# A linear-attention and mixer kernel: the order of the first batch, the pace of weight conversion, two clears and a small copy

## The chip, the cores and the metric

The kernel runs on one core of one Trainium2 chip. Its time is the device time of one execution in microseconds (us). The time before is the median of three executions; one further execution was taken by the profiler.

The engines go by their short names in the profile: PE is TensorE, PEld its weight loads, DVE VectorE, ACT ScalarE, POOL GpSimd, SP SyncE (here it only issues DMAs).

## The reference

Sizes: 4 batches, 8 heads, 768 steps, head dimension 48; model width 384, hidden width 1536, rank 32.

```python
f = 1.0 / (1.0 + np.exp(-f_logit))
for t in range(S):
    state = f[:, :, t, :, None] * state + np.einsum('bhd,bhe->bhde', k[:, :, t], v[:, :, t])
    y[:, :, t] = np.einsum('bhd,bhde->bhe', q[:, :, t], state)
# heads side by side: x has shape (batch, seq, 384)
h = x.transpose(0, 2, 1) @ U @ V
u = x + h.transpose(0, 2, 1)
out = u + np.maximum(u @ w_ch1, 0.0) @ w_ch2
```

The inputs q, k, v and f_logit are float32. The weights U, V, w_ch1 and w_ch2 are float64 and are turned into float32 on the chip.

## The kernel before

**Units.** The attention works in units of two heads; a batch has HP = 4 units, so units 0 to 3 are the first batch and there are NU = 16. A unit's 768 steps are 12 chunks of C = 64. Its front (`prepare`) makes decayed keys and queries; its rear (`attend`) has the pieces `kept` (transposes of the keys, L899, copied by ScalarE, L903), `spread` (the chunks' decays repeated, L909), `states` (sums of keys and values by chunk, L920, copied by ScalarE, L927), `scan` (the states one after the other, a VectorE scan, L942), `scores` (L872) and `mask` (VectorE, L885), `read` (queries by states into y, L959), and `inner` (masked scores by values into the same y, L977; then ScalarE copies y into x, L983).

**The two kinds of front.** In the first batch the five pieces of the front are: `gates` = logarithms (VectorE floor L730, ScalarE exp and ln L732 and L733), `read_back` = sums of them on TensorE (`log_sums`, L739), `keep` = three exponentials and a copy on ScalarE (L752 to L757), then `keys` and `queries` (transposes on TensorE, L709, and a VectorE product, L721). From unit 4 on, `gates` is a sigmoid (L763 or L771), `keep` a backward VectorE scan (L776) with a few 12-column operations behind it (L781 to L786), `read_back` a forward scan (L794). These scans read `fz`, in which the first column of each chunk and one more column at the end must be zero, and `starts`, which holds one value at the first column of each chunk and zeros elsewhere. In the first batch `fz` serves as scratch (its exponentials are kept there).

**Order.** TensorE, VectorE and ScalarE run the pieces in the order in which the code calls them, each engine in its own queue; up to `written.close()` SP's loads are in written order too. In the loop over n in the first batch a list of pieces is put together for each unit and called through. One call of a piece queues its instructions on every engine it uses. Two PSUM pools limit how far TensorE runs ahead: `ps_big` (3 buffers of two banks: transposes, scores, states, y, and the mixing products) and `ps_mm` (2 buffers of one bank: the mixer's products `pz` and `po`, and the low-rank products `ph`).

**Weights.** `weight_loader` gives four functions for each tile of float64 weights: the first issues its DMA; `halves` makes two ScalarE operations (L91, L92); `join` three VectorE operations (L98, L99, L100) and one GpSimd addition that writes the float32 tile (L101). `weights` holds U, two pieces of V (early = 3), 12 tiles of w_ch1 (called tiles 0 to 11 here) and 12 of w_ch2. `ahead_by` couples them: converting weight number i first issues the DMA of number i + 10.

**The mixer of the first batch.** After unit 3 come the low-rank products in two parts (`done`: the columns of units 0 to 2; `rest`: those of unit 3), the additions to x (`mix_of`, VectorE L197), transposes of x (`turn_of`, L279, L255), and 18 pieces `ch1` of 12 recorded matmuls each (L293, L267) that end in a ScalarE relu (L310). Piece (j, a) needs the w_ch1 tiles 2j and 2j + 1. The loop below runs the later pieces, converts weight tiles after each, and from i = 3 on adds one attention piece of the second batch:

```python
        for t in [starts] + fz:
            nc.vector.memset(t, 0.0)
        ...
        for i, (_, piece) in enumerate(start + m.firsts[1:]):
            piece()
            for f in loads[: (2, 1, 2, 1, 1, 0)[i] if i < 6 else 1]:
                loads.remove(f)
                f()
            if i >= EARLY:
                next(second)()
```

`busy` issues matmuls on a zero tile into a bank that nothing reads (L1068).

Of the kernel before, what the change touches and what calls it, by code (L numbers as in the profile page):

```python
# [111 lines left out]
def ahead_by(n, loads):  # L112


    def call(i):
        if i + n < len(loads):
            loads[i + n][0]()
        loads[i][1]()

    return [lambda i=i: call(i) for i in range(len(loads))]  # L120
# [396 lines left out]
def factored_path(ctx, tc, q, k, v, f_logit, moe_U, moe_V, moe_w_ch1, moe_w_ch2, out, ok):  # L517
# [4 lines left out]
    nc = tc.nc  # L522
    B, H, S, D = q.shape
    P = nc.NUM_PARTITIONS
    C = P // 2
# [111 lines left out]
    nc.vector.memset(ends, 0.0)  # L637
    nc.vector.memset(ends.rearrange("p (c t) -> p c t", t=C)[:, :, C - 1], 1.0)
    starts = other[:, 3, :]
    fz = [const.tile([P, S + 1], F32, name=f"fz{i}") for i in range(2)]  # L640

    kz = [const.tile([P, C + S], F32, name=f"kz{i}") for i in range(2)]
# [2 lines left out]
    least = const.tile([P, NU, NCH], F32, name="least")  # L645
# [14 lines left out]
    early = len(weights)  # L660
# [18 lines left out]
    def backwards(t, first, n):  # L679

        a = t[:, first : first + 1]
        return bass.AP(a.tensor, a.offset, [list(a.ap[0]), [-1, n]])
# [9 lines left out]
    def prepare(n):  # L692
# [4 lines left out]
        r, f = raw[n % 2], fz[n % 2]  # L697
# [76 lines left out]
        def keep():  # L774
            X = T["X"] = late[:, 4, :]
            nc.vector.tensor_tensor_scan(  # L776
                backwards(X, S - 1, S), backwards(f, S, S), backwards(ends, S - 1, S), 0.0,
                ALU.mult, ALU.add,
            )
            X0 = X.rearrange("p (c t) -> p c t", t=C)[:, :, 0]  # L780
            nc.scalar.copy(least[:, n, :], X0)  # L781
            X1 = two.tile([P, NCH], F32, name="X1")
            nc.vector.tensor_single_scalar(X1, X0, LEAST, ALU.max)
            nc.vector.reciprocal(starts.rearrange("p (c t) -> p c t", t=C)[:, :, 0], X1)
            whole = wholes[n % 2]
            nc.vector.tensor_tensor(whole[:, 1:NCH], T["f0"][:, 1:NCH], X0[:, 1:NCH], ALU.mult)  # L786
# [19 lines left out]
    def mixer(b):  # L806
        return Mixer(tc, b, x_tiles[b], U, V, w1, w2, sums if b else None, ident, blocks, out, two, three, zp, ps_big, ps_mm,
                     b == 0, z_all, room if b >= B - 2 else None, FEWER - (b - B + 2) * NCH // 4)
# [184 lines left out]
    def front(n, *names):  # L993

        if n >= NU:
            return []
        if n not in ahead:
            ahead[n] = dict(zip(("gates", "keep", "keys", "read_back", "queries"), prepare(n)))
        return [ahead[n].pop(nm) for nm in names]

    def rear(n, *names):

        if not 0 <= n < NU:
            return []
        if n not in here:
            here[n] = dict(zip(("kept", "states", "scan", "scores", "read", "inner", "mask", "spread"), attend(n)))
        return [here[n].pop(nm) for nm in names if nm in here[n]]
# [23 lines left out]
    def attention(pieces, portions, todo):  # L1031

        fill = Fill(todo, portions)
        for piece in pieces:
            fill()
            piece()
        fill.rest()

    def beside(pieces, n, calls):

        for i, piece in enumerate(pieces):
            yield piece
            for f in calls[:2] if i >= n else []:
                calls.remove(f)
                f()
        assert not calls
# [14 lines left out]
    with tc.manual_schedule(engines={nc.vector.engine, nc.scalar.engine}):  # L1061


        idle = ps_mm.tile([P, 512], F32, name="idle", tag="mm")

        def busy(n, cols=DM):
            for _ in range(n):
                nc.tensor.matmul(idle[:, 0:cols], lhsT=blank[:, 0:P], rhs=blank[:, 0:cols], start=True, stop=True)  # L1068

        written = ExitStack()  # L1070
        written.enter_context(tc.manual_schedule(engines={nc.sync.engine}))
        busy(3)
        for piece in front(0, "gates", "read_back", "keep"):
            piece()
        load(1, "k", "q")
        load(2, "f")
        load(1, "v")
        loads = ahead_by(early + FIRST + 1, weights)
        halves, join = [[w[i] for w in weights[:early]] for i in (2, 3)]
        done, rest = slice(0, 2 * (HP - 1) * D), slice(2 * (HP - 1) * D, DM)  # L1080

        def held():
            for i in range(2, FIRST, 2):
                t = zp.tile([P, NFC // 2, 2 * P], F32, name="zw").rearrange("p i t -> p (i t)")
                nc.scalar.copy(t[:, 0:1], x_tiles[0][:, 0, 0:1])
                spare.extend([t.bitcast(U64)[:, 0:WP], t.bitcast(U64)[:, WP : 2 * WP]])
            for load_w in weights[early + 2 : early + FIRST]:
                load_w[0]()
            load(HP, "f", "k", "q", "v")

        for n in range(HP):
            last = n + 1 == HP
            pieces = rear(n - 1, "scan") + (join[:1] if last else []) + front(n, "keys") + rear(n, "spread")
            pieces += rear(n - 1, "read") + front(n, "queries") + rear(n, "kept")
            if n == 0:
                pieces += [lambda: busy(1, 2 * P)] + front(1, "gates") + rear(0, "scores", "mask", "states")
            elif last:
                pieces += halves[1:2] + join[1:2] + rear(n - 1, "inner") + [held] + rear(n, "scores", "mask")
                pieces += halves[2:] + rear(n, "states", "scan") + join[2:]
            else:  # L1100
                pieces += rear(n - 1, "inner") + front(n + 1, "gates") + rear(n, "scores", "mask", "states")
            if n + 2 == HP:
                pieces += halves[:1]
            if not last:
                pieces += front(n + 1, "read_back", "keep")
            for piece in pieces:
                piece()
            if n == 0:
                load(2, "k", "q")
                load(3, "f")  # L1110
                load(2, "v")
            elif n == 1:
                weights[0][0]()
                load(3, "k", "q")
                for load_w in weights[1:early]:
                    load_w[0]()
                load(3, "v")
                for load_w in weights[early : early + 2]:
                    load_w[0]()
        m = mixer(0)  # L1120
        low_rank_of, added_up_of, mix_of, turn_of, ch1_of = m.some
        for load_w in weights[early + FIRST : early + FIRST + 4]:
            load_w[0]()
        load(HP + 1, "f", "k", "q", "v")
        written.close()
        low_rank_of(done)
        busy(2, 2 * P)
        loads[early]()
        for piece in rear(n, "read"):
            piece()  # L1130
        loads[early + 1]()
        added_up_of(done)
        for piece in rear(n, "inner"):
            piece()
        mix_of(done, range(0, NBL - 2, 2))
        low_rank_of(rest)
        mix_of(done, range(NBL - 2, NBL, 2))
        added_up_of(rest)
        turn_of(0, range(2))
        mix_of(rest)  # L1140
        ch1_of(0, 0, (0, 0), (0, 1))
        turn_of(0, range(2, NDC))
        ch1_of(0, 0, (1, 0), (1, 1))
        m.before[4][1]()
        ch1_of(0, 0, (0, 2), (1, 2))
        loads = loads[early + 2 :]
        loads.pop(0)()
        for t in [starts] + fz:
            nc.vector.memset(t, 0.0)

        start = m.before[5:]

        EARLY = 3
        second = chain(front(HP, "gates", "keep", "keys", "read_back", "queries"), steps(HP, 2 * HP + 1))
        for i, (_, piece) in enumerate(start + m.firsts[1:]):
            piece()
            for f in loads[: (2, 1, 2, 1, 1, 0)[i] if i < 6 else 1]:
                loads.remove(f)
                f()
            if i >= EARLY:  # L1160
                next(second)()
        for f in loads:
            f()
        n = len(m.seconds) // (NBL // 2)
        todo, after = m.seconds[:-n], m.seconds[-n:]

        attention(second, 12 + 10 * HP - (len(start) + len(m.firsts) - 1 - EARLY), todo)
        m = start_mixer(1, after)
        for f in to_sum:
            f()  # L1170
# [5 lines left out]
    pieces = beside(steps((B - 1) * HP + 1, NU + 1), 10 * (HP - 2), [lambda i=i: sum_of_w(i) for i in range(len(W_SUMS))])  # L1176
# [374 lines left out]
```

## Time and profile before

| | us |
|---|---|
| median of 3 executions (lowest, highest) | 484.69 (483.83, 487.08) |
| the profiled execution | 483.4 |
| its span, first to last instruction | 481.7 |
| PE busy | 462.5 (96%) |
| PEld busy | 399.2 (83%) |
| DVE busy | 345.8 (72%) |
| ACT busy | 180.7 (38%) |
| POOL busy | 36.1 (7%) |

A busy row counts an engine's instructions, not its waits. In a timeline line the two numbers in front are start and duration in us; what stands in square brackets is how long the engine sat idle before, and what released it. A line of the waits is: engine and operation that waited, what it waited for, total us, times, longest. A line of the stretches is: from and to, length, busy us of PE, PEld, DVE, ACT and POOL with instruction counts, the granted TensorE clock (1.00 is full), the DMA share and GB/s. A line of the DMA issues ends with the KB of each and the median us from issue to landing.

### The profile page before, as it was taken

Reading aid. Unit: us, or ns where it says so; the run is one execution under the profiler, and the core shown is the slowest. Engines: PE = TensorE matmul, PEld = TensorE weight load, DVE = VectorE, ACT = ScalarE, POOL = GpSimd, SP = SyncE. Lnnn points to the kernel's source line nnn. Section 1 sums busy time; section 2 is a strip of 40 time slices with the busy share of each in tenths; the row PEclk is TensorE's granted clock in tenths of the full one; section 3 lists DMA queues with packets and bytes.
Section 4 is the critical chain, followed back from the end, with each engine's and each line's share of the span. In section 5 each row is a group of like instructions: output and inputs, shape, how many; then the busy total and the mean of one; then the engine's idle time right before and its main releaser. Section 6 shows DMA issues by size and latency. Waiting matters only on the chain.

```text
span 481.7 us, 12787 instructions
## 1 busy us (share of the span) xinstructions
PE 462.5 (96%) x5551; PEld 399.2 (83%) x5551; DVE 345.8 (72%) x557; ACT 180.7 (38%) x339; POOL 36.1 (7%) x48
## 2 busy tenths in 40 slices
PE   7899979998999899999999999999999999999995
PEld 5786868885666468799899888899979999999995
DVE  4567686798999755757766646997896886858642
ACT  5675665663444313424342414542321311212200
POOL 2002254443000000000000000000000000000000
PEclk9999999998999999999999999999999999999999
DMA  9979996657787521253426200100000000000001
GB/s 145 153 134 252 217 207 130 157 134 108 109 125 113 95 42 26 26 75 72 64 28 114 43 30 4 29 3 20 17 1 1 33 2 18 18 0 34 1 33 39
DMA packets 158679, 34.34 MB, mean 71 GB/s; under 512 B 149206, under 2 KB 157078, under 8 KB 158614
## 3 DMA queue, kind: packets, MB, share of 16 engines
q1 hardware_dynamic: 158614, 33.44, 37.6%
q8 instruction: 45, 0.74, 0.7%
q14 instruction: 20, 0.16, 0.1%
HBM read 28.70 MB, written 4.72 MB: 69 GB/s over the span
## 4 chain that ended last, share of the span: by engine, by line
PE 77%; DVE 11%; ACT 3%; issue 3%; SPq 2%; DMA 2%; POOL 1%; DVEq 0%; POOLq 0%; ACTq 0%
PE pw L356 26%; PE pz L267 18%; PE pp L454 12%; PE po L327 4%; PE y L959 3%; PE y L977 2%; PE sc L872 2%; PE ds L920 2%; PE pt L899 2%; PE pt L709 1%; PE put L255 1%; SPq L592 1%; DVE w_y L99 1%; DVE late L794 1%; PE pu L207 1%
## 5 line engine op out<-in xcount | busy, mean ns | idle before, releaser
L267 PE MATMUL pz<-uT,w 128*128 128x256 f32 x492 | 112.2, 383 | 3.8 <-ACT z_all L310 3.7
L267 PEld LDWEIGHTS pz<-uT,w 128*128 128x128 f32 x492 | 91.5, 190 | 17.9 <-ACT z_all L310 4.2
L356 PE MATMUL pw<-w,z_all 128*128 128x192 f32 x216 | 37.7, 329 | 0.0
L356 PE MATMUL pw<-zw,w_raw 128*128 128x192 f32 x216 | 37.3, 327 | 0.0
L356 PEld LDWEIGHTS pw<-zw,w_raw 128*128 128x128 f32 x216 | 35.2, 190 | 0.7 <-DVE w_raw L197 0.6
L356 PEld LDWEIGHTS pw<-w,z_all 128*128 128x128 f32 x216 | 35.0, 190 | 0.7
L101 POOL TENSOR_TENSOR w<-w_y,w_r 128x384 int32<-128x384 int32 x24 | 31.5, 1314 | 43.7 <-DVE w_y L100 43.7
L310 ACT ACTIVATE z_all<-pz 128x512 f32<-128x512 f32 x33 | 19.6, 597 | 33.1 <-PE pz L267 33.0
L454 PE MATMUL pp<-v_nat,late 128*128 128x128 f32 x224 | 28.8, 275 | 0.0
L327 PE MATMUL po<-w,zw 128*128 128x384 f32 x72 | 25.3, 496 | 2.0 <-POOL w L101 2.0
L454 PEld LDWEIGHTS pp<-v_nat,late 128*128 128x128 f32 x224 | 27.0, 192 | 0.0
L447 ACT ACTIVATE other<-other 128x512 f32<-128x512 f32 x18 | 11.3, 631 | 39.9 <-DVE other L197 39.9
L947 ACT COPY st<-added 128x576 f32<-128x576 f32 x12 | 14.7, 1225 | 30.5 <-DVE added L942 30.5
L327 PE MATMUL po<-w,z_all 128*128 128x384 f32 x72 | 25.0, 495 | 1.2 <-DVE o L197 1.2
L885 DVE TENSOR_TENSOR A<-sc,causal 128x768 f32<-128x768 f32 x16 | 15.2, 951 | 13.4 <-PE sc L872 13.4
L776 DVE TENSOR_TENSOR_SCAN late<-fz,late 128x768 f32<-128x768 f32 x12 | 21.1, 1755 | 4.0 <-ACT fz L771 3.6
L327 PEld LDWEIGHTS po<-w,zw 128*128 128x128 f32 x72 | 13.1, 190 | 11.6 <-POOL w L101 2.6
L327 PEld LDWEIGHTS po<-w,z_all 128*128 128x128 f32 x72 | 13.4, 192 | 10.1 <-DVE o L197 1.8
L98 DVE TENSOR_SCALAR w_y<-w_y 128x384 f32<-128x384 f32 (+3 forms) x27 | 11.1, 410 | 14.3 <-ACT w_y L91 14.2
L794 DVE TENSOR_TENSOR_SCAN late<-fz,other 128x768 f32<-128x768 f32 x12 | 21.0, 1747 | 0.2
L927 ACT COPY added<-ds 48x576 f32<-48x576 f32 (+1 forms) x28 | 17.8, 635 | 5.8 <-PE ds L920 5.7
L447 ACT ACTIVATE z_all<-z_all 128x512 f32<-128x512 f32 x12 | 7.6, 630 | 32.8 <-DVE z_all L197 32.8
(219 smaller groups left out, 853.8 us busy)
## 6 DMA issues: line engine op xcount, KB each, us to landing
w_raw<-in_moe_w_ch_dram SPq DMA_DIRECT2D x18, 384.0 KB, 3.9
out_dram<-o SPq DMA_DIRECT2D x24, 192.0 KB, 1.9
v_nat<-in_v_dram SPq DMA_DIRECT2D x16, 144.0 KB, 3.8
v_nat<-in_v_dram SPq DMA_DIRECT2D x32, 72.0 KB, 3.8
zw<-in_moe_w_ch_dram SPq DMA_DIRECT2D x6, 384.0 KB, 5.6
late<-in_f_logit_dram SPq DMA_DIRECT2D x10, 96.0 KB, 3.1
late<-in_k_dram SPq DMA_DIRECT2D x10, 96.0 KB, 2.7
late<-in_q_dram SPq DMA_DIRECT2D x10, 96.0 KB, 2.5
```

The lines of the kernel that those rows point to most:

```text
L101: nc.gpsimd.tensor_tensor(dst.bitcast(I32), shaped(y.bitcast(I32)), shaped(r), ALU.add)
L267: nc.tensor.matmul(pm[:, i * 2 * P : (i + 1) * 2 * P], lhsT=w1[:, m, o : o + P], rhs=uT[a][:, m, :], start=(m == 0), stop=(m == NDC - 1))
L310: nc.scalar.activation(z[a, c][:, k : k + 2, :].rearrange("p i t -> p (i t)"), pm, AF.Relu)
L327: nc.tensor.matmul(pm, lhsT=z[a, i // NI][:, i % NI, s * P : (s + 1) * P], rhs=w2[:, i, :], start=(i == 0), stop=(i == NFC - 1))
L356: nc.tensor.matmul(pm[:, n * HM : (n + 1) * HM], lhsT=lhs[:, i, :], rhs=rhs[:, i, :], start=(i == 0), stop=(i == NI - 1))
L447: nc.scalar.activation(dst, dst, AF.Relu, scale=float(SIGNS[n]))
L454: nc.tensor.matmul(pm[:, i, r * P : (r + 1) * P], lhsT=room["w"](wn)[:, r * P : (r + 1) * P], rhs=x_node(a, xn), start=((xn, wn) == of[0]) ...
L776: nc.vector.tensor_tensor_scan(backwards(X, S - 1, S), backwards(f, S, S), backwards(ends, S - 1, S), 0.0, ALU.mult, ALU.add,)
L794: nc.vector.tensor_tensor_scan(Y, f[:, 0:S], starts, 0.0, ALU.mult, ALU.add)
L885: nc.vector.tensor_tensor(T["A"], sc[:, :, 0 : NBL * C].rearrange("p h (c i) -> p h c i", i=C), causal.unsqueeze(1).unsqueeze(1).broadcast ...
L927: nc.scalar.copy(added[r, 1:].rearrange("p (e c s) -> p e c s", c=NBL, s=2), ds[r, :, 0 : NBL * D].rearrange("p s (c e) -> p e c s", e=D),)
L947: nc.scalar.copy(st, states.rearrange(by_e, c=NCH))
```

## The change

It has seven parts.

1. `starts` is cleared once near the beginning of the program (L639).
2. Later, at L1148, only the columns of `fz` that must be zero are cleared: 12 strided columns and one at the end, for each of the two tiles.
3. The copy of the backward scan's first values (`X0`, L781) is a VectorE operation instead of a ScalarE one.
4. Units 1 and 2: the next unit's `gates` come before the previous unit's `inner`; `states` come before `scores` and `mask`; the unit's `scan`, `scores` and `mask` are called between the next unit's `read_back` and `keep`. Before, `scan` opened the next unit's list.
5. Unit 3: the join of U moves from ahead of the keys to behind the queries; the halves of V's second piece, the states, the scan and the last join come before the scores and the mask.
6. Around the low-rank products, the first conversion (tile 0) is called ahead of `low_rank_of(done)`, and the four `busy` matmuls there are gone.
7. In the loop over the mixer's pieces, i = 0 converts two tiles and every later i one, instead of 2, 1, 2, 1, 1, 0 for the first six.

```diff
@@ -637,6 +637,7 @@
     starts = other[:, 3, :]
+    nc.vector.memset(starts, 0.0)
@@ -778,7 +779,7 @@
             X0 = X.rearrange("p (c t) -> p c t", t=C)[:, :, 0]
-            nc.scalar.copy(least[:, n, :], X0)
+            nc.vector.tensor_copy(least[:, n, :], X0)
@@ -1090,19 +1091,21 @@
         for n in range(HP):
             last = n + 1 == HP
-            pieces = rear(n - 1, "scan") + (join[:1] if last else []) + front(n, "keys") + rear(n, "spread")
-            pieces += rear(n - 1, "read") + front(n, "queries") + rear(n, "kept")
+            pieces = rear(n - 1, "scan") + front(n, "keys") + rear(n, "spread") + rear(n - 1, "read")
+            pieces += front(n, "queries") + (join[:1] if last else []) + rear(n, "kept")
             if n == 0:
                 pieces += [lambda: busy(1, 2 * P)] + front(1, "gates") + rear(0, "scores", "mask", "states")
             elif last:
-                pieces += halves[1:2] + join[1:2] + rear(n - 1, "inner") + [held] + rear(n, "scores", "mask")
-                pieces += halves[2:] + rear(n, "states", "scan") + join[2:]
+                pieces += halves[1:2] + join[1:2] + rear(n - 1, "inner") + [held] + halves[2:]
+                pieces += rear(n, "states", "scan") + join[2:] + rear(n, "scores", "mask")
             else:
-                pieces += rear(n - 1, "inner") + front(n + 1, "gates") + rear(n, "scores", "mask", "states")
+                pieces += front(n + 1, "gates") + rear(n - 1, "inner") + rear(n, "states")
             if n + 2 == HP:
                 pieces += halves[:1]
             if not last:
-                pieces += front(n + 1, "read_back", "keep")
+                pieces += front(n + 1, "read_back")
+                pieces += rear(n, "scan", "scores", "mask") if n else []
+                pieces += front(n + 1, "keep")
@@ -1123,9 +1126,8 @@
         written.close()
+        loads[early]()
         low_rank_of(done)
-        busy(2, 2 * P)
-        loads[early]()
         for piece in rear(n, "read"):
             piece()
         loads[early + 1]()
@@ -1145,8 +1147,9 @@
         loads.pop(0)()
-        for t in [starts] + fz:
-            nc.vector.memset(t, 0.0)
+        for t in fz:
+            nc.vector.memset(t[:, 0:S].rearrange("p (c t) -> p c t", t=C)[:, :, 0], 0.0)
+            nc.vector.memset(t[:, S : S + 1], 0.0)
@@ -1154,7 +1157,7 @@
             piece()
-            for f in loads[: (2, 1, 2, 1, 1, 0)[i] if i < 6 else 1]:
+            for f in loads[: 2 if i == 0 else 1]:
```

## The prediction

> **What bounds the kernel now.** First I read the page's busy row, then TensorE's waits in three stretches of the span, then the table of stretches, then the timeline of the first 80 us by engine.
>
> ```profile
> span 481.7 us, 12787 instructions
> PE 462.5 (96%) x5551; PEld 399.2 (83%) x5551; DVE 345.8 (72%) x557; ACT 180.7 (38%) x339; POOL 36.1 (7%) x48
> ```
>
> TensorE is the bound of the whole: 462.5 of 481.7 us. A change that leaves its matmuls alone can only take TensorE's idle time, or add some. The idle time that matters is listed by the waits between 50 and 125 us, and its place by the stretches:
>
> ```profile
> PE pz L267 <- ACT z_all L310: 2.6, 3, 1.3
> PE po L327 <- POOL w L101: 2.0, 1, 2.0
> ```
>
> ```profile
> 50.00:60.00 10.00, 9.86 (x52) 8.44 (x51) 8.08 (x15) 6.85 (x15) 3.00 (x3) 1.00 0.88 221
> 60.00:70.00 10.00, 8.63 (x41) 6.79 (x39) 8.30 (x14) 6.48 (x12) 5.04 (x5) 1.00 0.99 201
> 70.00:80.00 10.00, 8.74 (x52) 7.50 (x53) 9.30 (x16) 6.18 (x13) 4.61 (x4) 1.00 0.70 152
> 80.00:90.00 10.00, 10.00 (x78) 8.62 (x80) 5.97 (x12) 5.67 (x14) 4.28 (x3) 1.00 0.61 146
> ```
>
> TensorE has holes from 60 to 80 us and none from 80 to 110. The timeline shows who makes them:
>
> ```profile
> 52.77 0.70 DVE L1149 MEMSET other<- 128x768 f32 x1
> 53.58 1.51 DVE L1149 MEMSET fz<- 128x769 f32 x2
> 56.43 0.99 POOL L101 TENSOR_TENSOR w<-w_y,w_r 128x384 int32<-128x384 int32 x1 [2.62 <-DVE w_y L100]
> ...
> 70.50 0.21 ACT L781 COPY least<-late 128x12 f32<-128x12 f32 x1 [2.63 <-DVE late L776]
> 70.61 1.08 ACT L310 ACTIVATE z_all<-pz 128x512 f32<-128x512 f32 x2
> 71.26 2.86 PE L267 MATMUL pz<-uT,w 128*128 128x256 f32 x12 [1.29 <-ACT z_all L310]
> ```
>
> Three clears hold VectorE from 52.77 to 55.09; then weight tiles follow each other every 1.95 us (a POOL join of 1.0, a VectorE part that waits for it). ScalarE's relus (L310, their waits in the list), which free the two one-bank PSUM buffers, stand in its queue behind those tiles' halves, and at 70.5 behind a 12-column copy that waits 2.63 us for a scan. The first 40 us have another limit, the loads:
>
> ```profile
> 21.14 0.55 PE L920 MATMUL ds<-v_nat,kb 64*64 64x48 f32 x19 [1.36 <-issue]
> 31.23 0.85 PE L709 MATMUL pt<-ident,other 128*128 128x128 f32 x6
> 36.41 0.96 DVE L885 TENSOR_TENSOR A<-sc,causal 128x768 f32<-128x768 f32 x1
> 36.66 1.18 PE L920 MATMUL ds<-v_nat,kb 64*64 64x48 f32 x48 [0.32 <-ACT zw L1085]
> 38.55 1.36 DVE L942 TENSOR_TENSOR_SCAN st<-added,whole 128x576 f32<-128x576 f32 x1 [1.18 <-ACT added L927]
> ```
>
> ```profile
> other<-in_k_dram SPq DMA_DIRECT2D x4, 144.0 KB, 4.6
> v_nat<-in_v_dram SPq DMA_DIRECT2D x8, 72.0 KB, 4.5
> ```
>
> Unit 3's second k load is issued at 26.50; with the median 4.6 us it lands at about 31.1, and its transposes start at 31.23. Its last v load is issued at 32.3; plus 4.5 is 36.8, and the states product (L920) runs from 36.66 to 37.84, 1.18 us where the same product of unit 2 took 0.87. Both wait for data. The mask (L885) runs in the gap ahead of the scan (L942).
>
> **What the Trainium skill says.** "Runtime: NRT & Kernel Launch", Instruction fetch mechanics: each engine's instructions are refilled in blocks of 256, by a DMA that is mostly hidden. Here one isn't: the 1.36 us before 21.14 has no releaser, and between 17.4 and 20 us the DMA view shows one 16 KB transfer of the instruction queue. "SBUF — State Buffer", SBUF: two separate sides: VectorE and GpSimd share a port pair that one instruction holds whole. The trace agrees: L99 takes 0.36 us alone and 1.05 beside a POOL join; a join takes 1.00, but 2.31 beside a scan. "TensorE: Matmul & The Clock Gate", The HAM clock gate: an idle window of about 3.4 us halves the clock. Here a shorter hole did: after 1.95 us idle at 114.6 the clock of 110 to 120 us is 0.88.
>
> **The change part by part.** Everything is set against the profiled execution: 483.4 us, of which the span is 481.7. That run is 1.3 us (0.27%) below the median of 484.69, so I carry the difference to the median.
>
> *Clear of starts at L639.* One 0.70 us memset moves to the start. VectorE ends its clears there at 2.94 and then idles 1.85 us until the first gates land at 4.78: nothing. Without that cover it would cost 0.70.
>
> *Unit order in the first batch.* In units 1 and 2 the next unit's logarithms (exp and ln, 0.69 and 0.68) go ahead of the x copy (0.64) on ScalarE, and the 48 score matmuls (0.72) move from a place beside that copy to one after the next log sums (L739). TensorE's cycle loses 0.64 and gains 0.72: a draw. One PSUM buffer is also tighter (log sums, scores and k transposes are all held when y is wanted, some 0.3 us a unit). The fetch stall of 1.36 us falls on an instruction that now runs later, and vanishes. But all of this runs up against unit 3's k at 31.2: early work waits there. Gain 0; from +0.5 to -0.5.
>
> *Unit 3.* Scores and mask go behind the scan. The states product still waits for v until 36.7 to 37.0, so scan L942 stays at 38.55 to 39.91. The mask (0.96) was done at 37.37, in VectorE's 1.18 us hole before the scan; now it is queued after it, ahead of weight tiles 0 and 1 and of the additions to x. V's join (0.76) lies there in both. VectorE has no hole from 38.55 to 46.0, and TensorE's transposes of x (45.01) wait for the first addition. L99 of tile 0 gets back 0.1: +0.85 us. It is 0 if v lands a microsecond sooner, +1.0 if nothing is got back. U's join (0.95) moves from ahead of the keys to after the queries, where VectorE idles; U is needed at 37.8.
>
> *Low rank.* The four filler matmuls (1.13) go; TensorE still waits for y's scan at 39.91: 0. Tile 0's halves (1.0) are now ahead of the copy of h on ScalarE: h is ready at 40.6 instead of 39.4, needed after y at 41.2: 0, and up to +0.5 if y comes sooner. SP issues tile 10's load one call sooner; it waits for its buffer as before.
>
> *Clears at L1148.* Out go 2.3 us of VectorE. In come four clears of 12 or 1 columns; L638's 12-column clear takes 0.07, so 0.3. Tiles 3 and on are joined 1.75 to 2.0 us sooner.
>
> *One tile a piece.* Pieces are numbered by the loop's i. Tile 7 moves from piece 2 to 3, 8 from 3 to 4, 9 from 4 to 5. So one pair of halves (1.0) fewer stands ahead of the relus of pieces 3, 4 and 5 on ScalarE. The same 19 tiles are issued by the last piece.
>
> *The copy of X0 on VectorE.* ScalarE no longer stops for the scan. Laid out by hand from 50.69 with these durations, joins of tiles 3 to 7 end at 55.6, 57.4, 59.2, 61.0 and 62.8 (before: 57.4, 59.4, 61.3, 63.3 and 65.2), and relus 3, 4 and 5 run at 58.6, 62.4 and 64.5 instead of 62.28, 66.39 and 70.61. TensorE then needs 7 pieces of 2.59 and 3 transposes of 0.66, 20.1 us, where it took 23.9 (50.69 to 74.61). That takes away the holes 0.64, 0.70 and 1.29 and the smaller losses around them: -3.75. Next late would be kz of unit 4, ready at about 70 and needed at 73.5. Bounds: -2.0 (only the clears' time comes back) to -3.8. On VectorE each copy adds its start spacing of about 0.15 (L783's median is 0.17). That counts where VectorE sets the pace. From 116 to 166 it is 90% busy and a TensorE wait of 1.2 on its addition (L197) ends at 166.3; five units' copies lie before it: 0.75 us, of 0 to 0.85. I take 0.7. The other seven are under TensorE's full queue.
>
> Sum: 0.85 - 3.75 + 0.7 = -2.2 us. The wait at 114.6 for the last w2 tile stays: its tile is released by the last relu, which moves along with TensorE.
>
> **The rivals.**
> 1. *More comes.* v lands sooner, the mask is hidden (0), the copies cost nothing, and the hole at 114.6 falls across two clock windows, so the half clock (3.4 us at half speed, 1.7) goes too: -3.75 - 1.7 = -5.4, 479.3 us. For it: the load stream has gaps. Against: all three must hold.
> 2. *Absorbed.* TensorE arrives 3 us sooner at 114.6 and 166 and waits there for the joins and additions: 484.7. For it: VectorE is over 90% busy after 110. Against: its queue there is paced by TensorE's relus before 106.
> 3. *Slower: VectorE becomes the bound.* The mask in the full queue costs 0.96 and the twelve copies 0.17 each (2.0), while the holes at 60 to 71 turn into waits for joins: +3.0, 487.7. It decides once less than 3.0 of the 3.75 comes back. For it: VectorE's 93% between 70 and 80. Against: 2.0 us of clears leave just before.
>
> **How the numbers follow.** Forecast 0.52, rival 1 0.16, rival 2 0.20, rival 3 0.12. The predicted time is 484.69 - 2.2 = 482.5; its own range from the bounds is 481 to 484.2. Reaching into the others to hold 8 in 10: 479.4 to 486.5. A measurement of this kernel tells about 1% (4.8 us) from no change. Only rival 1 ends below 479.8: faster 0.15. Rival 3 would have to grow by half to pass 489.5, with what I overlooked 0.07. Same is 0.78.
>
> **What would show it.** Right: no L310 wait of TensorE between 60 and 75, piece 8's products (74.6 before) at 71 to 72, the scan of unit 3 still near 38.5 with the mask behind it, and the first x addition at 44.8. Wrong, if the scan of unit 3 starts before 37.5, if TensorE still waits over 1 us for L310 or L101 before 80, or if the wait before 166 grows beyond 2 us.

## The result and the profile after

| | before | after |
|---|---|---|
| median of 20 executions each, us | 484.25 | 481.39 |
| ratio, 95% interval | | 0.9934 (0.9918 to 0.9950) |
| span of the profiled execution, us | 481.7 | 478.5 |
| PE, DVE, ACT busy, us | 462.5, 345.8, 180.7 | 461.5, 346.4, 179.1 |

The changed kernel is 0.66% faster: the interval lies wholly below 1, and the gain is less than the 1% that was called a difference. Three of its 20 executions were slow (487.49 to 489.09 us) and are left out of the ratio; over all runs here 10 of 134 executions with the new order of the first batch were slow, and none of 180 with the old one.

From L639 to the loop over n (L1090) the lines have moved down by one: the copy of `X0` is L782, the mask L886, the scan of the states L943.

The busy row of the page after:

```profile
span 478.5 us, 12782 instructions
PE 461.5 (96%) x5547; PEld 399.2 (83%) x5547; DVE 346.4 (72%) x571; ACT 179.1 (37%) x327; POOL 36.1 (8%) x48
```

PE's 1.0 us less is about what the four filler matmuls took (1.13), and these stood where TensorE had to wait anyway. What counts is its idle time. TensorE's waits from 50 to 125 us, after:

```profile
PE po L327 <- POOL w L101: 2.0, 1, 2.0
```

The line with three waits for L310 (2.6 us) is gone; the wait for the last w2 tile stands. The stretches after (columns as before):

```profile
50.00:60.00 10.00, 10.00 (x54) 8.85 (x53) 7.94 (x18) 8.02 (x16) 3.70 (x4) 1.00 0.91 223
60.00:70.00 10.00, 10.00 (x51) 8.83 (x50) 8.25 (x17) 7.42 (x14) 4.60 (x4) 1.00 0.90 193
70.00:80.00 10.00, 10.00 (x63) 8.60 (x62) 9.72 (x15) 6.68 (x13) 5.33 (x4) 1.00 0.66 155
80.00:90.00 10.00, 10.00 (x95) 8.61 (x94) 8.55 (x17) 5.65 (x11) 4.92 (x4) 1.00 0.74 179
```

TensorE is full from 50 to 90, where it had 9.86, 8.63, 8.74 and 10.00. The timeline after shows why:

```profile
50.93 7.94 PE L267 MATMUL pz<-uT,w 128*128 128x256 f32 x36
52.86 0.07 DVE L1151 MEMSET fz<- 128x12 f32 x1
52.87 0.06 DVE L1152 MEMSET fz<- 128x1 f32 x1
55.39 1.00 POOL L101 TENSOR_TENSOR w<-w_y,w_r 128x384 int32<-128x384 int32 x1 [1.35 <-DVE w_y L100]
59.29 0.58 ACT L310 ACTIVATE z_all<-pz 128x512 f32<-128x512 f32 x1
63.41 0.60 ACT L310 ACTIVATE z_all<-pz 128x512 f32<-128x512 f32 x1
64.78 0.61 ACT L310 ACTIVATE z_all<-pz 128x512 f32<-128x512 f32 x1
71.03 2.76 PE L267 MATMUL pz<-uT,w 128*128 128x256 f32 x12
```

The clears last 0.1 us together, the join of tile 3 ends at 56.39 where it ended at 57.42, and the relus of pieces 3, 4 and 5 run at 59.29, 63.41 and 64.78 where they ran at 62.28, 66.39 and 70.61. No matmul group between 50 and 125 us carries an idle time for L310 any more. Piece 1 starts at 50.93 and piece 8 at 71.03: 20.10 us. Before it was 23.92, as the timeline of before shows, with the marks that are compared below:

```profile
43.94 2.08 DVE L197 TENSOR_TENSOR x<-x,pu 128x576 f32<-128x576 f32 x3
50.69 8.35 PE L267 MATMUL pz<-uT,w 128*128 128x256 f32 x36
74.61 2.76 PE L267 MATMUL pz<-uT,w 128*128 128x256 f32 x12
116.45 0.91 PE L327 MATMUL po<-w,zw 128*128 128x384 f32 x2 [1.95 <-POOL w L101]
166.29 4.14 PE L327 MATMUL po<-w,z_all 128*128 128x384 f32 x12 [1.17 <-DVE o L197]
```

Unit 3 in the timeline after:

```profile
35.80 1.58 PE L921 MATMUL ds<-v_nat,kb 64*64 64x48 f32 x47 [0.50 <-ACT w_r L92]
38.15 1.36 DVE L943 TENSOR_TENSOR_SCAN st<-added,whole 128x576 f32<-128x576 f32 x1 [1.16 <-ACT added L928]
40.11 0.94 DVE L886 TENSOR_TENSOR A<-sc,causal 128x768 f32<-128x768 f32 x1
44.18 2.07 DVE L197 TENSOR_TENSOR x<-x,pu 128x576 f32<-128x576 f32 x3
```

The mask now stands behind the scan. The first addition to x starts 6.03 us after the scan's start, where it was 5.39 (43.94 less 38.55).

The third place that moved is TensorE's wait on VectorE's addition at 163, behind the wait for the last w2 tile, after:

```profile
112.87 0.91 PE L327 MATMUL po<-w,zw 128*128 128x384 f32 x2 [1.96 <-POOL w L101]
163.12 4.14 PE L327 MATMUL po<-w,z_all 128*128 128x384 f32 x12 [1.64 <-DVE o L197]
```

Before, these waits were 1.95 and 1.17. The spans now add up: scan of unit 3 sooner, -0.40 (38.15 against 38.55); from it to piece 1, +0.64 (12.78 against 12.14); piece 1 to piece 8, -3.82; piece 8 to the end of this wait, +0.41 (92.09 against 91.68); behind it the same 315.4. The sum is -3.17 of 3.2.

### The profile page after: what moved, and what is told of

It reads as the page before. It is cut to its first block, busy times and chain, and to the rows that moved or that the text cites. A ratio compares the mean times of both kernels' runs of the same rounds, so it can differ in the third digit from the quotient of the medians.

```text
span 478.5 us, 12782 instructions
## 1 busy us (share of the span) xinstructions
PE 461.5 (96%) x5547; PEld 399.2 (83%) x5547; DVE 346.4 (72%) x571; ACT 179.1 (37%) x327; POOL 36.1 (8%) x48
## 4 chain that ended last, share of the span: by engine, by line
PE 79%; DVE 9%; DMA 3%; SPq 3%; ACT 2%; issue 2%; POOL 0%; DVEq 0%; ACTq 0%; POOLq 0%
PE pw L356 26%; PE pz L267 22%; PE pp L454 12%; PE po L327 4%; PE sc L873 2%; DMA v_nat<-in_v_dram 2%; PE y L960 2%; PE y L978 2%; PE put L255 2%; PE ds L921 1%; PE pt L900 1%; PE pt L710 1%; SPq L592 1%; DVE late L795 1%; PE pu L207 1%
## 5 line engine op out<-in xcount | busy, mean ns | idle before, releaser
L310 ACT ACTIVATE z_all<-pz 128x512 f32<-128x512 f32 x33 | 19.7, 598 | 42.6 <-PE pz L267 42.5
L948 ACT COPY st<-added 128x576 f32<-128x576 f32 x12 | 14.7, 1225 | 39.7 <-DVE added L943 39.7
L886 DVE TENSOR_TENSOR A<-sc,causal 128x768 f32<-128x768 f32 x16 | 15.2, 951 | 12.2 <-PE sc L873 12.1
L98 DVE TENSOR_SCALAR w_y<-w_y 128x384 f32<-128x384 f32 (+3 forms) x27 | 12.3, 456 | 11.1 <-ACT w_y L91 11.1
L928 ACT COPY added<-ds 48x576 f32<-48x576 f32 (+1 forms) x28 | 17.8, 636 | 4.9 <-PE ds L921 4.8
```

The lines of the kernel that those rows point to most:

```text
L310: nc.scalar.activation(z[a, c][:, k : k + 2, :].rearrange("p i t -> p (i t)"), pm, AF.Relu)
L886: nc.vector.tensor_tensor(T["A"], sc[:, :, 0 : NBL * C].rearrange("p h (c i) -> p h c i", i=C), causal.unsqueeze(1).unsqueeze(1).broadcast ...
L928: nc.scalar.copy(added[r, 1:].rearrange("p (e c s) -> p e c s", c=NBL, s=2), ds[r, :, 0 : NBL * D].rearrange("p s (c e) -> p e c s", e=D),)
L948: nc.scalar.copy(st, states.rearrange(by_e, c=NCH))
```

## The experiments

The theory: the gain is the stage of weight conversion alone, each of three edits takes a different wait away there, the order of the first batch brings nothing, and the copy on VectorE costs a part of it later. The rivals: one edit makes the gain and the others ride along; or the order itself brings it.

The ratio of every run but the one marked is taken against executions of the kernel before on the same chip (medians 483.64 to 483.96 there). The stretches come from one profiled execution of each kernel. "Stage" is piece 1 to piece 8; "head" is the start of unit 3's scan to piece 1; "long stretch" is from the end of the wait for the last w2 tile to the end of the wait for VectorE's addition: 166.29 less 116.45, 49.84 us, before, and 163.12 less 112.87, 50.25 us, after.

### Parts of the stage, one at a time

Clears alone (before, with parts 1 and 2):

```diff
+    nc.vector.memset(starts, 0.0)
-        for t in [starts] + fz:
-            nc.vector.memset(t, 0.0)
+        for t in fz:
+            nc.vector.memset(t[:, 0:S].rearrange("p (c t) -> p c t", t=C)[:, :, 0], 0.0)
+            nc.vector.memset(t[:, S : S + 1], 0.0)
```

> The kernel before with the two clears alone (starts at the beginning, 13 columns of fz each). Theory A (the gain comes from the weight stage, each of its three edits gives a part): the joins of tiles 3 on come 1.75 to 2 us sooner, the TensorE waits before pieces 5 and 6 go, but ScalarE still stops for the scan and piece 7 waits 1.4 us; TensorE reaches piece 8 about 2.3 us sooner than before (72.3 in place of 74.6), time about 2.3 us less. Rival B (the order of the first batch gives the gain): no more than 0.5 us less.

Measured: 482.99 us, 0.9985 (0.9965 to 1.0004), no difference that the time can show. Stage 22.65, so 1.27 less. Its timeline:

```profile
59.59 5.38 PE L267 MATMUL pz<-uT,w 128*128 128x256 f32 x24
66.33 2.83 PE L267 MATMUL pz<-uT,w 128*128 128x256 f32 x12 [0.70 <-ACT z_all L310]
70.46 2.86 PE L267 MATMUL pz<-uT,w 128*128 128x256 f32 x12 [1.30 <-ACT z_all L310]
```

Only the first wait (0.64) has gone; 0.70 and 1.30 are still there. That the clears' 2.3 us come back as 2.3 was wrong. The operation behind the clears is the first of tile 3 (L98), here it is before:

```profile
55.00 0.30 DVE L98 TENSOR_SCALAR w_y<-w_y 128x384 f32<-128x384 f32 x1
```

And here it is with the clears taken out, beside the GpSimd join of tile 2:

```profile
53.28 1.00 POOL L101 TENSOR_TENSOR w<-w_y,w_r 128x384 int32<-128x384 int32 x1 [7.64 <-DVE fz L1151]
53.38 1.12 DVE L98 TENSOR_SCALAR w_y<-w_y 128x384 f32<-128x384 f32 x1 [0.19 <-ACT w_y L91]
```

Counted from piece 1 it starts 2.09 us sooner (2.22 against 4.31), but beside that join it takes 1.12 instead of 0.30. So tile 3's join ends only 1.27 sooner (5.46 against 6.73 behind piece 1), and the two waits that are left end 1.27 sooner as well.

Copy alone (before, with part 3):

```diff
-            nc.scalar.copy(least[:, n, :], X0)
+            nc.vector.tensor_copy(least[:, n, :], X0)
```

> The kernel before with the copy of X0 on VectorE alone. Theory A: only the last of the three waits, 1.29 us ahead of piece 7, goes; piece 8 starts about 1.4 us sooner; the wait at 165 (1.17) grows by 0.4 to 0.7, time about 0.8 us less. Rival B: nothing in the stage, only the later loss: 0.5 us more.

Measured: 482.64 us, 0.9978 (0.9960 to 0.9997). Stage 22.34, 1.58 less. Its timeline:

```profile
63.49 2.86 PE L267 MATMUL pz<-uT,w 128*128 128x256 f32 x12 [0.62 <-ACT z_all L310]
67.71 5.42 PE L267 MATMUL pz<-uT,w 128*128 128x256 f32 x24 [0.71 <-ACT z_all L310]
```

Here it is the third wait (1.29) that has gone: the relu that stood behind the copy. The wait at 165 grew to 1.64, as expected.

One tile a piece alone (before, with part 7):

```diff
-            for f in loads[: (2, 1, 2, 1, 1, 0)[i] if i < 6 else 1]:
+            for f in loads[: 2 if i == 0 else 1]:
```

> The kernel before with one weight tile a piece alone. Theory A: the waits ahead of pieces 5 and 6 (0.64 and 0.70) go, the one ahead of piece 7 stays at about 1.3; piece 8 about 1.7 us sooner, time 1.7 less. Rival B: 0. The three parts' gains are not to be added: together they can take no more than the 3.7 us that TensorE loses there.

Measured: 481.65 us, 0.9957 (0.9929 to 0.9985). Stage 22.01, 1.91 less. Its timeline:

```profile
58.84 5.35 PE L267 MATMUL pz<-uT,w 128*128 128x256 f32 x24
64.68 2.75 PE L267 MATMUL pz<-uT,w 128*128 128x256 f32 x12
68.67 2.86 PE L267 MATMUL pz<-uT,w 128*128 128x256 f32 x12 [1.23 <-ACT z_all L310]
```

The first two waits have gone, the copy's stays. The three edits alone make 1.27 + 1.58 + 1.91 = 4.76 us; together they make 3.82. The clears and the pace both take the first wait, yet these two add up: the kernel with the copy back on ScalarE (below) has them both, with the new order, which alone leaves the stage at 23.93. Its stage is 20.72, 3.20 less than before, and 1.27 + 1.91 is 3.18. It is the copy that brings less in company, 0.62 instead of 1.58. So no single edit is the gain: it is one queue with three obstacles, each seen in its own line. The long stretch tells which edit costs something later: 49.84 with the clears, 49.85 with the pace, 50.25 with the copy.

### The order of the first batch

Order alone (the changed kernel with parts 1, 2, 3 and 7 undone):

```diff
-                pieces += halves[1:2] + join[1:2] + rear(n - 1, "inner") + [held] + rear(n, "scores", "mask")
-                pieces += halves[2:] + rear(n, "states", "scan") + join[2:]
+                pieces += halves[1:2] + join[1:2] + rear(n - 1, "inner") + [held] + halves[2:]
+                pieces += rear(n, "states", "scan") + join[2:] + rear(n, "scores", "mask")
...
+        loads[early]()
         low_rank_of(done)
-        busy(2, 2 * P)
-        loads[early]()
```

> The kernel before with the order of the first batch alone (units 1 to 3, tile 0 ahead of the low rank, no filler matmuls), old clears, old copy, old pace. Theory A: the states of unit 3 wait for v either way and the mask stands behind the scan, so piece 1 starts 0.2 to 0.8 us later than 50.69 and all three waits stay: time 0.2 to 0.8 us more. Rival B: this is the part that gains: 2 us or more less.

Measured: 484.42 us, 1.0006 (0.9991 to 1.0021). Stage 23.93. The scan started at 39.03 and the head was 12.78: the 0.64 us are the order's. The time neither shows nor excludes them; its interval goes from 0.4 us less to 1.0 us more.

All but the order (before, with parts 1, 2, 3 and 7: the three diffs above in one kernel):

```diff
+    nc.vector.memset(starts, 0.0)
...
+            nc.vector.tensor_copy(least[:, n, :], X0)
...
+            for f in loads[: 2 if i == 0 else 1]:
```

> The changed kernel with the first batch in its old order (clears, copy and pace alone). Theory A: piece 1 at 50.7, piece 8 at 70.8, the wait at 162 as in the changed kernel (1.6); time 0.2 us below the changed kernel, 3.4 below before. Rival B: most of the gain is lost, 1 us or less below before.

Measured: 480.46 us, 0.9909 (0.9874 to 0.9943). Stage 20.10, head 12.14. The whole gain is there without the order: the rival that credits the order falls. That it is better than the changed kernel isn't shown, since the intervals overlap (0.9874 to 0.9943, from six executions, and 0.9918 to 0.9950).

Mask first (the changed kernel, unit 3's scores and mask ahead of the states again):

```diff
-                pieces += halves[1:2] + join[1:2] + rear(n - 1, "inner") + [held] + halves[2:]
-                pieces += rear(n, "states", "scan") + join[2:] + rear(n, "scores", "mask")
+                pieces += halves[1:2] + join[1:2] + rear(n - 1, "inner") + [held] + rear(n, "scores", "mask")
+                pieces += halves[2:] + rear(n, "states", "scan") + join[2:]
```

> The changed kernel with unit 3's scores and mask ahead of its states again. My step: the mask behind the scan holds up VectorE's queue (tile joins 0 and 1, additions to x). If so the first addition to x starts about 0.5 to 0.9 us sooner than 44.18 and piece 1 at 50.2 to 50.5. Rival: the scan starts 0.4 us later again (38.5), as before, and takes the same back: piece 1 at 50.7 to 50.9, no change.

Measured: 481.31 us, 0.9929 (0.9905 to 0.9953). In its timeline mask, scan and the first addition follow each other so:

```profile
38.09 0.95 DVE L886 TENSOR_TENSOR A<-sc,causal 128x768 f32<-128x768 f32 x1
38.95 1.35 DVE L943 TENSOR_TENSOR_SCAN st<-added,whole 128x576 f32<-128x576 f32 x1
44.33 2.08 DVE L197 TENSOR_TENSOR x<-x,pu 128x576 f32<-128x576 f32 x3
```

Scan to addition is 5.38 again, and the head 12.13, so the 0.64 come from the mask behind the scan. Piece 1 all the same starts at 51.08, which neither expectation had (50.2 to 50.5, or 50.7 to 50.9), since the scan starts 0.80 later than in the changed kernel. The mask, now ahead of it, is at most 0.1 of that: the copy that the scan needs (L928) ended at 38.85, 0.10 before the scan. The unit came late as a whole; its k transposes started at 32.27, against 31.05. The times of the two orders can't be told apart (0.9929 and 0.9934). Over the profiles the scan started between 37.72 and 40.19 in the five kernels with the old order, and between 37.96 and 40.77 in the eight with the new one, this kernel apart: the start scatters by more than the 0.64.

### Where the copy belongs

Copy back on ScalarE (the changed kernel with part 3 undone):

```diff
-            nc.vector.tensor_copy(least[:, n, :], X0)
+            nc.scalar.copy(least[:, n, :], X0)
```

> The changed kernel with the copy of X0 on ScalarE again. Theory A: with clears and pace in place the scan of unit 4 ends at 67.5, ScalarE stops there ahead of the relu of piece 5 (64.8 in the changed kernel), and piece 7 waits about 0.8 to 1.5 us; the wait at 161.8 goes back from 1.64 to 1.2. Time 0.3 to 1.0 us more than the changed kernel. Rival: the copy is hidden once the scan is sooner: 0.4 us less than the changed kernel.

Measured: 481.35 us, 0.9949 (0.9928 to 0.9970). Stage 20.72, with one wait left:

```profile
69.06 2.86 PE L267 MATMUL pz<-uT,w 128*128 128x256 f32 x12 [0.35 <-ACT z_all L310]
```

The wait is shorter than the 0.8 to 1.5 expected, though the scan that the copy waits for ended where it was expected, 16.6 us behind piece 1: TensorE comes to piece 7 only 0.35 us before the relu behind that copy is done. With one tile a piece alone the clears still stood ahead of the scan, which ended 17.9 behind piece 1, and the wait was 1.23. This is why the copy brings less in company. The wait at 164 fell back to 1.17 and the long stretch to 49.83. So the copy on VectorE brings 0.62 in the stage and costs 0.42 later: beside the other two edits it is no gain that a time can show (0.9949 without it, 0.9934 with it, the intervals overlap).

Copy on GpSimd:

```diff
-            nc.vector.tensor_copy(least[:, n, :], X0)
+            nc.gpsimd.tensor_copy(least[:, n, :], X0)
```

> The changed kernel with the copy of X0 on GpSimd, which is idle after 120 us. If the growth of the wait before 162 (1.17 to 1.64) comes from the copies in VectorE's queue, it goes back to about 1.2, no relu waits for a scan, and the time is 0.4 to 0.6 us below the changed kernel. Rival: the growth has another cause (TensorE arrives sooner): the wait stays at 1.6, no change.

Measured: 481.70 us, 0.9943 (0.9925 to 0.9961). Stage 20.10, as on VectorE. The wait at 164 is 1.62, not the 1.2 expected, and the long stretch 50.11. The rival foresaw the 1.6, but its reason, that TensorE arrives sooner, fails: with the clears or the pace alone TensorE arrives sooner too, and the stretch stays at 49.84 and 49.85. The timelines of one unit, first the changed kernel, then this one:

```profile
135.11 1.76 DVE L777 TENSOR_TENSOR_SCAN late<-fz,late 128x768 f32<-128x768 f32 x1 [0.90 <-ACT fz L772]
136.91 0.17 DVE L782 COPY least<-late 128x12 f32<-128x12 f32 x1
136.99 0.17 DVE L784 TENSOR_SCALAR X<-late 128x12 f32<-128x12 f32 x1
```

```profile
137.00 1.76 DVE L777 TENSOR_TENSOR_SCAN late<-fz,late 128x768 f32<-128x768 f32 x1 [0.97 <-ACT seen L967]
138.79 0.17 DVE L784 TENSOR_SCALAR X<-late 128x12 f32<-128x12 f32 x1
138.82 0.21 POOL L782 COPY least<-late 128x12 f32<-128x12 f32 x1 [11.91 <-DVE late L777]
```

On VectorE the copy holds the next operation back by 0.08 us only (136.99 less 136.91), so there was no more than 0.4 in five units to win. On GpSimd VectorE is spared that, but sits idle for 0.97 us instead of 0.90 ahead of each scan. Where those 0.07 come from was not settled.

Copy on VectorE for units 4 and 5, on ScalarE from unit 6 (one profiled execution, 485.39 us; its start was late, so only its stretches are read):

```diff
+            (nc.vector.tensor_copy if n < HP + 2 else nc.scalar.copy)(least[:, n, :], X0)
```

> The changed kernel with the copy on VectorE for units 4 and 5 alone, on ScalarE from unit 6 on. The copies lengthen VectorE's period by 0.08 us a unit, and on GpSimd by 0.06, since the next scan then waits for it. With ScalarE's the distance between the ends of the two waits (111 and 162) goes back from 50.3 to 49.8, and piece 8 stays 20.1 us behind piece 1. Rival: it stays at 50.2 or more.

Measured: long stretch 49.85, wait at its end 1.18, as expected. So the copies from unit 6 on are the whole of the cost. All ten profiles that have the wait for the last w2 tile and the copy on ScalarE or VectorE agree: 49.83 to 49.85 in the six with the later copies on ScalarE, 50.24 to 50.25 in the four with them on VectorE.

### The wait for the last w2 tile

Two weight tiles also at pieces 9 and 12, copy on VectorE:

```diff
-            for f in loads[: 2 if i == 0 else 1]:
+            for f in loads[: 2 if i in (0, 9, 12) else 1]:
```

> The changed kernel with two tiles also at pieces 9 and 12, so that no w_ch2 tile is left for after the last piece. VectorE has idle time there (1.2 us before 81.5, 2.4 before 92.9). If the wait of 1.96 at 111 is for the last tile alone, it goes; the joins of 107 to 110 are gone from ahead of unit 6's scan, so the whole stretch that VectorE paces up to 162 starts up to 3.3 us sooner: time 2 to 3.5 us below the changed kernel. Rival: the wait is only moved, to the one before 162 or to pieces 10 to 14, since VectorE has the same work to do: within 0.5 us of the changed kernel.

Measured: 482.67 us, 0.9960 (0.9941 to 0.9978): not better than the changed kernel, where 2 to 3.5 us less were expected. The wait at 112 has gone, and TensorE's waits from 80 to 172 us read:

```profile
PE pz L267 <- ACT zw L310: 3.1, 1, 3.1
PE po L327 <- DVE o L197: 1.4, 1, 1.4
```

The timeline of this run shows the chain of the wait of 3.1:

```profile
93.74 1.35 DVE L943 TENSOR_TENSOR_SCAN added<-added,whole 128x576 f32<-128x576 f32 x1
95.12 1.20 ACT L948 COPY st<-added 128x576 f32<-128x576 f32 x1 [2.25 <-DVE added L943]
96.35 0.60 ACT L310 ACTIVATE zw<-pz 128x512 f32<-128x512 f32 x1
97.09 1.19 PE L267 MATMUL pz<-uT,w 128*128 128x256 f32 x2 [3.06 <-ACT zw L310]
```

The extra tile delays unit 4's scan of the states on VectorE; ScalarE stops for it with its copy (L948), and the relu that frees TensorE's buffer stands behind that. It is the copy of `X0` over again, in another place. In this execution the wait cost more than its length: from 98 to 100 us the granted clock was 0.50, and the 24 matmuls behind the wait took 7.01 us, where they took 5.42 in the next kernel, at full clock behind a wait of 3.03.

Both together (this and the split copy):

```diff
+            (nc.vector.tensor_copy if n < HP + 2 else nc.scalar.copy)(least[:, n, :], X0)
...
+            for f in loads[: 2 if i in (0, 9, 12) else 1]:
```

> Both: two tiles also at pieces 9 and 12, and the copy on ScalarE from unit 6 on. If both reasons hold the gains add: 2.5 to 4 us below the changed kernel, 476 to 479 us. Rival (the work of VectorE is only moved): within 0.7 us of the changed kernel.

Measured: 481.17 us, 0.9953 (0.9926 to 0.9981), with the same wait of 3.0 at 94. The 476 to 479 expected were missed. In the trace, piece 8 to the end of the wait for the addition (162.47 less 71.89) is 90.58 us where the changed kernel has 92.09; the times don't show these 1.5 us.

One tile more at piece 9 only, with the split copy:

```diff
+            (nc.vector.tensor_copy if n < HP + 2 else nc.scalar.copy)(least[:, n, :], X0)
...
+            for f in loads[: 2 if i in (0, 9) else 1]:
```

> The changed kernel with the copy of X0 on VectorE for units 4 and 5 and on ScalarE from unit 6 on, and with a second weight tile at piece 9 alone (so one w_ch2 tile, not two, is left for the end of the batch). Theory (VectorE's queue between 81 and 112 sets the wait at 112; one tile fits into its idle time before the scan of unit 4, two don't): no wait of 3 us at 94; the wait of TensorE near 112 shrinks from about 2 us to 0.6 or less; the copies give 0.47 us of the stretch up to 164; together 1.5 to 2.4 us below the changed kernel, 479 to 480 us. Rival (the wait only moves, as it did with two tiles): at least 1.5 us of wait turns up elsewhere before 170 and the time lies within 0.5 us of the changed kernel's 481.4.

Measured: 480.48 us, 0.9939 (0.9922 to 0.9956), beside 0.9934 of the changed kernel against the same kernel before: no difference that can be shown. TensorE's waits from 80 to 125 us in its profile:

```profile
PE pz L267 <- ACT zw L310: 1.1, 1, 1.1
```

The wait of 2.0 at 112 has gone, one of 1.1 has come at 99 on the same chain, and piece 8 to the end of the wait for the addition (168.58 less 77.45) is 91.13 us where the changed kernel has 92.09. So about 1 us of the 1.5 to 2.4 expected is seen in the trace, 0.4 of it from the split copy, which alone has 91.70, and the rival is half right. (The profiled execution itself had a half clock from 44 to 55 and took 486.13 us, so nothing before piece 1 is read from it.) No version that is shown to beat the changed kernel was found.

## Why the prediction was right, point by point

Predicted were 482.5 us, 2.2 less than before; measured were 481.39, 2.86 less than its own before, and 3.2 less in the spans. Of the 0.97 by which the spans gained more than the sum said, 0.40 is chance (the scan's start), 0.21 the size of unit 3, 0.29 that of the copies and 0.07 the stage. The range "481 to 484.2" isn't what the bounds give: unit 3, the stage and the copies at their ends make 480.9 to 484.5, and with the first-batch order and the low rank 480.4 to 485.5.

- *Clear of starts, low rank* (0 each): no trace of either in the sum of the spans.
- *Unit order in the first batch* (0, and the fetch stall of 1.36 vanishes): right. After, TensorE has no idle time marked "issue" at the states of unit 1, and unit 3's k transposes start at 31.05 (31.23 before): the early part still ends at the load of k.
- *Unit 3* (+0.85): the place was right, the size not. The head grew by 0.64, in the changed kernel and with the order alone. The mask, 0.94 long, holds the next operation back by 0.87 (40.98 less 40.11), and the term "L99 of tile 0 gets back 0.1" was too small: tile 0's three operations take 1.25 (40.98 to 42.23) instead of 1.49 (40.51 to 42.00). The scan's own start, which I held at 38.55, was 38.15; that 0.4 lies within the scatter of the runs and is luck.
- *Clears, one tile a piece, copy off ScalarE* (-3.75): right, the stage took the 20.1 us that were predicted, and the single runs show that each edit removes what the list says. One step of it failed: "Tiles 3 and on are joined 1.75 to 2.0 us sooner". They came 1.03 sooner (tile 3 at 56.39, forecast 55.6; tile 7 at 64.20, forecast 62.8), because L98 of tile 3 took 1.10 beside the join of tile 2. For the same reason the bound of -2.0 for "only the clears' time comes back" was too large: the clears taken alone bring 1.27. The relus forecast at 58.6, 62.4 and 64.5 came at 59.29, 63.41 and 64.78. The sum did not suffer, as 20.1 us is what TensorE's own work takes without a wait: the relus had time to spare.
- *The copy on VectorE* (+0.7): mis-sized. The long stretch grew by 0.41. The term that failed is "its start spacing of about 0.15 (L783's median 0.17)": that is a duration, and the next operation starts 0.08 after the copy. Five units make 0.4.
- *The wait at 114.6 stays*: it did, 1.96 at 112.9. It is VectorE's, and in the three kernels that take a tile from there another wait comes in its place (3.1, 3.0 and 1.1).
- *Rival 1, more comes*: fell on its own term. The half clock was to give 1.7 us. With one tile a piece alone the clock is full there and in the changed kernel it isn't, by the stretches of the two:

```profile
110.00:120.00 10.00, 8.04 (x126) 5.01 (x125) 9.83 (x12) 4.11 (x8) 2.85 (x2) 1.00 0.63 90
```

```profile
110.00:120.00 10.00, 8.04 (x122) 5.48 (x121) 9.86 (x13) 3.15 (x4) 2.31 (x1) 0.83 0.56 78
```

  Both have TensorE busy for 8.04 and VectorE for over 9.8; from here to the addition the kernel before, with its clock of 0.88, needs 49.84 us and the kernel with one tile a piece, at 1.00, 49.85. VectorE sets that stretch, so the clock costs nothing there.
- *Rival 2, absorbed*: its place was right (0.41 is lost before 163), its size was not. VectorE's work before 112 had moved along with TensorE, as the argument against it said.
- *Rival 3, VectorE becomes the bound*: its point of decision was not reached, 3.82 of 3.75 came back.

Of the signs, the absence of a wait for L310 and the mask behind the scan held; piece 8 came at 71.03 (71 to 72 said), the first addition at 44.18 (44.8 said), and the wait before 166 was 1.64, under the 2 that would have spoken against it.

## What to carry to other kernels

Read a hole of TensorE through the queue of the engine that frees its buffer: what stands ahead of the freeing instruction there, and what does *that* wait for. Every wait here, the three that went and the ones that the experiments made, is a relu behind a ScalarE copy or conversion that stood waiting for VectorE, or for a GpSimd join behind VectorE. When several edits clear one queue, price them by laying the queue out once for all of them, as the sum of single gains (4.76) overstates what they give together (3.82): one edit can shorten the wait that another removes. And before filling an idle wait elsewhere with work, see whose scan that work delays.

## What the runs showed of the hardware

- A small VectorE operation that started beside a GpSimd join ended with the join. The timeline of the changed kernel from 65.76:

```profile
65.76 1.75 DVE L777 TENSOR_TENSOR_SCAN late<-fz,late 128x768 f32<-128x768 f32 x1
65.99 2.31 POOL L101 TENSOR_TENSOR w<-w_y,w_r 128x384 int32<-128x384 int32 x1 [1.79 <-DVE w_y L100]
67.54 0.79 DVE L782 COPY least<-late 128x12 f32<-128x12 f32 x1
68.25 0.16 DVE L784 TENSOR_SCALAR X<-late 128x12 f32<-128x12 f32 x1
```

  The join needs 2.31 instead of 1.00 beside the scan and ends at 68.30; the copy of 12 columns, 0.17 in the units without a join beside it, needs 0.79 and ends at 68.33. The same pair ends at 112.81 and 112.84 two units later. That fits the port pair that one instruction holds whole (the Trainium skill, "SBUF — State Buffer", SBUF: two separate sides), and the operation behind the copy takes 0.16, so it pays nothing of it.
- Idle time of TensorE marked "issue", which I had read as a fetch of instructions, showed up in some programs and not in others, at different places: 1.36 before 21.14 in the kernel before, 1.00 to 1.32 at the same matmuls in three kernels with its order, none in the changed kernel but 0.74 ahead of its first log sums, and 1.50 in the middle of unit 3's reads in the two kernels with the split copy and at most one tile more. That these are fetches is not shown: the kernel before has a 16 KB transfer of the instruction queue between 17.4 and 20 us, but the changed kernel has one between 17 and 22 us too, and no stall. I had counted on one stall going; where the next program puts its own was not to be seen in the profile.
- Five of the nine profiled kernels with the new order, where the four filler matmuls are gone, show a half clock for some microseconds between 37 and 55 us (the last one from 44 to 55; with a stall of 1.50 its head took 18.23 against 12.78), and none of the five with the old order does there, though one of these has it from 22 to 26. Whether the fillers prevent it was not tried: open.
